# Gate arithmetic on 128 partitions, two prefix scans, an own place for a chunk's queries, and a newly searched order in an mLSTM with two MLP layers

## The chip, the cores and the metric

One core of one Trainium2 chip. The core has TensorE (PE; its weight loads are listed as PEld), VectorE (DVE), ScalarE (ACT), GpSimd (POOL) and SyncE (SP), which issues the fetches from HBM. The metric is the device time of one execution in microseconds, the median of several runs. Lower is better.

## The reference, cut to what matters

An mLSTM recurrence over 768 steps for 2 x 8 heads of width 40, with a running maximum m over the gates, then two MLP layers (320 to 2048 to 320) on its 1536 tokens.

```python
for t in range(S):
    m_new = np.maximum(f_gate[:, :, t] + m, i_gate[:, :, t])
    f_stab = np.exp(f_gate[:, :, t] + m - m_new)
    i_stab = np.exp(i_gate[:, :, t] - m_new)
    m = m_new
    C = f_stab * C + i_stab * outer(v_t, k_t)
    n = f_stab * n + i_stab * k_t
    y[:, :, t] = sigmoid(o_t) * (C @ q_t) / max(|n . q_t|, 1)
...
h = x @ w_in;  x = (h * clip(h + 3, 0, 6) / 6) @ w_out          # first layer
h = x @ w_in;  out = (h * tanh(log1p(exp(h)))) @ w_out          # second layer
```

## The kernel before

**Attention.** The sequence is cut into six chunks c of 128 steps, each of two halves of 64. `scan_gates` runs the maximum m along a row per (batch, head), 16 rows in all, with one scan; it takes chunk 0 alone, chunk 1 alone and chunks 2 to 5 together (`SCANS`). It then forms f + m(before) and subtracts m(after) from both gates, on those 16 partitions, in the tile gio (for chunk 1 on GpSimd, `pool_scan`). `gates(c)` transposes the two results of a chunk with the identity (tile pg), takes exp as a ratio of two sigmoids (tile ist), transposes the forget factor back (pf) and forms its running product in each half of 64 with one scan over 128 elements (pr): at the first element of each half the factor is put to 0 and its value is kept in the tile first, so that the scan starts anew there. For chunks 0 and 1 the decays are spread to 128 partitions by products with the identity (fb); for the others by a way through HBM (fzd). Then come, per chunk, the products of scores (s, L815), of the state (st, L942), of the state with the queries (x, L890) and of the decayed scores with the values (z, L985); `mixture(c)` puts them together and transposes the result (xp, L1041) into the input X of the first layer. X has three parts of two chunks each; two are made at the start, the third takes over memory that chunks 1 and 3 had used.

**Layers.** Weights are fetched in eight slots per layer, an in half (ri, 768 KB) and an out half (ro, 640 KB), through four raw buffers; ScalarE, VectorE and GpSimd split each into a high and a low part (`narrow`, `prep`: wh, wl, wd). The first layer runs chunks 0 and 1 (of X part 0) slot by slot (`step1`: ph, acc), then the parts 1 and 2 in wide blocks of 512 columns (`step1_wide`: phw, accw). The second layer (`step2`: qh, bcc) follows.

**Order.** The order of instructions on every engine is fixed when the program is built. All work is written as tasks with priorities (the lists in `P`, lowest first). `Flow` plays them through with estimated durations: whichever engine or buffer is free first takes the ready task of lowest priority, and the order so found is the program's. A fetch takes its turn on SyncE, which holds at most eight in flight. While TensorE would wait in this plan, `keep_warm` puts in products of zeros (tile pz), until chunk 1's result is there. The queries of a chunk (qke) share one buffer, `in_qke`, which is given back when the chunk's cross products and scores are done. Values and keys (kvo) have one place for chunks 1 and 3 and one for the others.

Of the kernel before, what the change touches and what calls it, by code (L numbers as in the profile page):

```python
# [16 lines left out]
ALU = mybir.AluOpType  # L17
# [25 lines left out]
    "const": [22, 11, 148],  # L43
    "gates": [81, 93, 41, 162, 127, 206],
    "load": [96, 281, 100, 227, 58, 130],
    "score": [9, 84, 243, 262, 211, 292],
    "value": [1, 29, 209, 138, 45, 241],
    "carry": [106, 73, 77, 59, 249, 250],
    "unit": [19, 171, 75, 86, 244, 228],
# [8 lines left out]
    ],  # L58
    "down2": [
        143, 60, 82, 259, 114, 54, 57, 63, 229, 156, 74, 6, 18, 44, 179, 139, 226, 173, 116, 155, 87, 183,  # L60
        203, 25, 72, 122, 53, 111, 115, 2, 151, 109, 27, 157, 3, 266, 263, 198, 24, 205, 32, 12, 88, 80,
        177, 89, 136, 90,
    ],
    "wide1": [
        140, 284, 67, 14, 33, 237, 185, 276, 235, 256, 288, 287, 215, 225, 248, 204, 191, 291, 184, 142, 17,
        79, 125, 144, 165, 34, 153, 39, 196, 293, 195, 102,
    ],
    "down1w": [
        35, 68, 290, 7, 105, 47, 30, 120, 251, 200, 297, 219, 50, 76, 124, 212, 152, 269, 16, 65, 99, 49,
        283, 26, 51, 15, 98, 94, 123, 37, 95, 277,  # L70
    ],
    "drain": [13, 217, 133, 126, 121, 56, 21, 48, 137, 71],
    "now": [4, 5],
# [13 lines left out]
    "pool_scan": [1, 0],  # L87
    "pe_low": [1, 1, 0, 0, 0, 0, 0, 0, 0, 0, 0, 0],
    "spread": [1, 1, 0, 0, 0, 0],
    "decay": [182, 253, 178, 141, 158, 104],  # L90
    "gload": [236, 40, 164, 175, 92, 181],
    "cross": [163, 83, 258, 103, 238, 66],
    "within": [214, 161, 36, 107, 112, 8],
# [50 lines left out]
class Flow:  # L144
# [4 lines left out]
    TO_PE, SWITCH = 0.13, 0.12  # L149
    TICK, COLUMNS = 10.24 / 3, 4000  # L150
    DMA = dict(rings0=2.0, slow=13e3, fast=20e3, until=3.0, start=1.9, end=0.5)

    def __init__(self):

        self.port = {DVE: 0.0, POOL: 0.0}
        self.engines = {PE: Engine(0.2), DVE: Engine(0.13), ACT: Engine(0.14), POOL: Engine(0.1), SP: Engine(0.0)}
        self.places = list(self.engines.values())
        self.now = 0.0
        self.rings, self.landed = [2.0] * 16, []
        self.tick, self.columns, self.fast = 0, 0.0, False  # L160
        self.fill, self.live, self.mode = None, 0, 0
# [76 lines left out]
    def transfer(self, place, t, size, n, issue):  # L238

        d = self.DMA  # L240
        rate = d["slow"] if t < d["until"] else d["fast"]
        for i in range(n):
            self.rings[i] = max(self.rings[i], t + d["start"]) + size / n / rate
# [30 lines left out]
    def grant(self, task, place, first):  # L274
# [5 lines left out]
        else:  # L280
# [4 lines left out]
            elif r[0] == PE:  # L285
                while self.fill and place.free + 0.45 < first:
                    self.fill()
                    place.free = self.products(place.free, 0.214, 512)
                mode = r[3] if len(r) > 3 else 0
                start = first + (self.SWITCH if mode != self.mode else 0.0)  # L290
# [11 lines left out]
def mlstm_mlp_kernel(ctx, tc, qk, kvon, gates_io, w1i, w1o, w2i, w2o, eyes, consts, out):  # L302
# [145 lines left out]
    for j in range(len(BLOCKS) - 1):  # L448
        new_x()
# [198 lines left out]
    first = gpool.tile([16, L], F32, tag="first", name="first")  # L648
# [8 lines left out]
    def scan_gates(i, c0, c1):  # L657
# [6 lines left out]
        on = i and P["pool_scan"][i - 1]  # L664
        eng = G if on else V
        for o, x, y, op in ((fgt, fgt, mt[:, a:z], ALU.add), (igt, igt, mt[:, a + 1 : z + 1], ALU.subtract),
                            (fgt, fgt, mt[:, a + 1 : z + 1], ALU.subtract)):
            yield flow.elementwise(on, 0.06 + 0.14 * n, 128 * n)
            tt(eng, o[:, r], x[:, r], y, op)
        flow.set(scanned[i])  # L670

    def gates(c):
# [5 lines left out]
        yield PE, 0.21, 128  # L678
        T.transpose(p[:, 0:16], fgt[:, q], ident[:16, :16])
        T.transpose(p[:, 16:32], igt[:, q], ident[:16, :16])  # L680
        g = istab[c] = gpool.tile([128, 32], F32, tag=f"ist{c}", name=f"ist{c}")
        s = gpool.tile([128, 32], F32, tag=f"s{c}", name=f"s{c}")
        yield ACT, 0.16
        A.activation(s, p[:, 0:32], AF.Sigmoid, scale=-1.0)
        A.activation(g, p[:, 0:32], AF.Sigmoid)
        flow.put(in_a)
        yield DVE, 0.27
# [22 lines left out]
        begins = pr.rearrange("r (a t) -> r a t", a=2)  # L710
# [9 lines left out]
        ends = begins[:, :, HL - 1]  # L720
# [39 lines left out]
    def loads(c, before):  # L760
# [105 lines left out]
    def cross(c):  # L866
# [44 lines left out]
        flow.put(in_qke)  # L911
# [452 lines left out]
```

## Time and profile before

| what | us |
|---|---|
| median of 3 runs | 434.56 (434.45 to 435.74) |
| the profiled execution | 434.39 |
| its span, first to last instruction | 432.6 |
| TensorE busy | 424.8 |
| VectorE busy | 303.0 |
| ScalarE busy | 268.9 |
| GpSimd busy | 60.0 |

The span is what the trace covers; 1.8 us of the execution's own time lie around it. Busy time is counted per engine and overlaps between engines. Matmuls are pipelined, so that TensorE's records overlap and a full stretch reads as fully busy.

### The profile page before, as it was taken

The numbers are of one execution on the slowest core, as the hardware profiler recorded it, in microseconds if no ns is written. First come the engines' busy times: TensorE is split into PE (matmuls) and PEld (weight loads), VectorE is DVE, ScalarE is ACT, GpSimd is POOL, SyncE is SP. The second block draws the span as 40 slices with busy tenths as digits, with TensorE's granted clock in tenths as the row PEclk, the third lists the DMA queues.
The fourth block names the chain that finished last, engine by engine and source line by source line (L and its number), as shares of the span: only waits on it lengthen the run. The fifth ranks groups of instructions, "written<-read, shape, count | busy, mean of one in ns | idle before, by whom it ended". The sixth has DMA issues, their size and how long they took to land.

```text
span 432.6 us, 9063 instructions
## 1 busy us (share of the span) xinstructions
PE 424.8 (98%) x3779; PEld 369.6 (85%) x3779; DVE 303.0 (70%) x532; ACT 268.9 (62%) x472; POOL 60.0 (14%) x54
## 2 busy tenths in 40 slices
PE   8999899999999999999999999999999999999996
PEld 6867899999998888887778888999999999899985
DVE  4989999999787322637976547766666666666664
ACT  5656676644443334069888358766686666767664
POOL 4010101181220134123036210000000000000000
PEclk9999999999999999999999999999999999999999
DMA  7958644651702027000782000000010000100001
GB/s 275 392 210 319 232 176 125 189 198 51 239 3 100 0 64 297 4 1 6 265 293 105 2 0 2 0 2 0 2 61 1 2 0 2 46 17 0 2 0 61
DMA packets 10040, 40.44 MB, mean 93 GB/s; under 512 B 2128, under 2 KB 3824, under 8 KB 9232
## 3 DMA queue, kind: packets, MB, share of 16 engines
q1 hardware_dynamic: 10000, 39.87, 25.8%
q8 instruction: 29, 0.48, 0.4%
q14 instruction: 11, 0.09, 0.1%
HBM read 37.64 MB, written 2.23 MB: 92 GB/s over the span
## 4 chain that ended last, share of the span: by engine, by line
PE 91%; DVE 4%; DMA 1%; ACT 1%; issue 1%; POOL 0%; DVEq 0%; ACTq 0%; POOLq 0%
PE qh L465 20%; PE accw L482 12%; PE phw L465 12%; PE acc L482 7%; PE ph L465 7%; PE bcc L1167 6%; PE bcc L1166 6%; PE bcc L1165 6%; PE pz L1198 4%; PE x L890 2%; PE s L815 1%; PE st L942 1%; DMA ri<-in_w2i 1%; PE z L985 1%; PE xp L1041 1%; PE fb L840 1%
## 5 line engine op out<-in xcount | busy, mean ns | idle before, releaser
L465 PE MATMUL qh<-x,wh 128*128 128x512 f32 x288 | 89.5, 392 | 0.0
L1116 DVE SCALAR_TENSOR_TENSOR u<-u,qh 128x512 f32<-128x512 f32 (+1 forms) x49 | 33.1, 676 | 39.1 <-ACT u L1114 39.1
L465 PEld LDWEIGHTS qh<-x,wh 128*128 128x128 f32 x288 | 52.3, 188 | 8.7
L1167 PE MATMUL bcc<-wd,gl 128*128 128x320 f32 x192 | 59.4, 309 | 0.2 <-DVE gl L1122 0.2
L1166 PE MATMUL bcc<-wd,gh 128*128 128x320 f32 x192 | 59.3, 309 | 0.0
L1165 PE MATMUL bcc<-wd,gh 128*128 128x320 f32 x192 | 59.3, 309 | 0.0
L465 PE MATMUL phw<-x,wh 128*128 128x512 f32 x192 | 58.9, 394 | 0.0
L1112 ACT ACTIVATE u<-u,two 128x512 f32<-128x512 f32 (+1 forms) x49 | 35.0, 715 | 30.8 <-DVE u L1110 30.7
L482 PE MATMUL accw<-ghw,wd 128*128 128x512 f32 x160 | 53.5, 399 | 0.0
L549 DVE SCALAR_TENSOR_TENSOR rw<-rw,phw 128x512 f32<-128x512 f32 x32 | 21.9, 686 | 38.4 <-ACT rw L547 38.2
L465 PEld LDWEIGHTS phw<-x,wh 128*128 128x128 f32 x192 | 35.7, 188 | 8.1
L547 ACT ACTIVATE rw<-phw,half 128x512 f32<-128x512 f32 x32 | 22.0, 689 | 26.5 <-PE phw L465 26.4
L482 PE MATMUL accw<-glw,wd 128*128 128x512 f32 x96 | 38.2, 398 | 0.2 <-DVE glw L309 0.2
L465 PE MATMUL qh<-x,wl 128*128 128x512 f32 x96 | 37.9, 395 | 0.0
L1165 PEld LDWEIGHTS bcc<-wd,gh 128*128 128x128 f32 x192 | 36.1, 188 | 2.1
L1166 PEld LDWEIGHTS bcc<-wd,gh 128*128 128x128 f32 x192 | 36.1, 188 | 1.9
L1106 ACT ACTIVATE u<-qh 128x512 f32<-128x512 f32 (+1 forms) x49 | 28.7, 587 | 14.3 <-PE qh L465 14.2
L1167 PEld LDWEIGHTS bcc<-wd,gl 128*128 128x128 f32 x192 | 36.1, 188 | 0.4 <-DVE gl L1122 0.4
L1122 DVE SCALAR_TENSOR_TENSOR gl<-u,gh 128x512 fp32r<-128x512 f32 (+1 forms) x49 | 33.1, 675 | 3.4 <-ACT gh L1120 3.3
L482 PEld LDWEIGHTS accw<-ghw,wd 128*128 128x128 f32 x160 | 29.5, 188 | 6.5
L1110 DVE SCALAR_TENSOR_TENSOR u<-u 128x512 f32<-128x512 f32 (+1 forms) x49 | 33.4, 681 | 1.6
L465 PE MATMUL ph<-x,wh 128*128 128x256 f32 x192 | 34.2, 288 | 0.0
(153 smaller groups left out, 838.7 us busy)
## 6 DMA issues: line engine op xcount, KB each, us to landing
ri<-in_w1i SPq DMA_DIRECT2D x8, 768.0 KB, 6.4
qke<-in_qk SPq DMA_DIRECT2D x6, 1024.0 KB, 5.0
ri<-in_w2i SPq DMA_DIRECT2D x8, 768.0 KB, 6.1
kvo<-in_kvon SPq DMA_DIRECT2D x6, 968.0 KB, 7.6
ro<-in_w1o SPq DMA_DIRECT2D x8, 640.0 KB, 5.2
ro<-in_w2o SPq DMA_DIRECT2D x8, 640.0 KB, 5.0
fb<-fzd SPq DMA_DIRECT2D x4, 512.0 KB, 4.3
out<-ot SPq DMA_DIRECT2D x12, 160.0 KB, 1.8
```

The source lines that it names most:

```text
L465: T.matmul(ph, a, b, start=(i == 0), stop=(i == len(seq) - 1))
L482: T.matmul(acc[k], a, b, start=start, stop=stop, skip_group_check=True)
L547: A.activation(r, ph, AF.Relu, bias=half, scale=1.0 / 6.0)
L549: V.scalar_tensor_tensor(out=r, in0=r, scalar=1.0, in1=ph, op0=ALU.min, op1=ALU.mult)
L1106: A.activation(u, ph, AF.Exp)
L1110: V.scalar_tensor_tensor(out=u, in0=u, scalar=2.0, in1=u, op0=ALU.add, op1=ALU.mult)
L1112: A.activation(u, u, AF.Ln, bias=two)
L1116: V.scalar_tensor_tensor(out=u, in0=u, scalar=0.5, in1=ph, op0=ALU.subtract, op1=ALU.mult)
L1122: V.scalar_tensor_tensor(out=gl, in0=u, scalar=-2.0, in1=gh.bitcast(F32), op0=ALU.mult, op1=ALU.subtract)
L1165: T.matmul(acc, a, hi, start=st, stop=False)
L1166: T.matmul(acc, a, lo, start=False, stop=False)
L1167: T.matmul(acc, b, hi, start=False, stop=sp)
```

## The change

- The gate subtractions leave `scan_gates`. `gates(c)` now transposes f, i, m before and m after (four transposes instead of two), copies the two m to SBUF on ScalarE, and adds and subtracts them on VectorE on 128 partitions, reading PSUM. The `pool_scan` entry goes.
- The running product is two scans of 64 elements, each started with 1.0, over a tile of zeros (nothing); the copy into first and the memset go.
- Chunk 1's queries are fetched into the memory of X part 1 (tile x1) instead of the shared buffer. Only part 0 of X is made at the start; part 1 is made when chunk 1 is done.
- The first gates are a task of their own with priority 0, ahead of the identity.
- `Flow` plays fetches with other constants (rate, start, end, sizes), gives each filler product at least 0.25 us and has two switch times. All priority lists are new.

```diff
 P = {
-    "const": [22, 11, 148],
+    "const": [55, 264, 205],
...
-    "load": [96, 281, 100, 227, 58, 130],
+    "load": [11, 262, 266, 59, 218, 45],
...
-    "prep0": [55, 62, 166, 0, 85, 160, 168, 52, 192, 149, 271, 213, 230, 234, 289, 285],
-    "prep1": [218, 169, 274, 220, 280, 282, 10, 135, 20, 172, 232, 38, 261, 189, 210, 194],
+    "prep0": [128, 75, 176, 132, 42, 109, 177, 116, 246, 53, 271, 261, 282, 274, 278, 280],
+    "prep1": [281, 273, 203, 187, 257, 138, 36, 193, 222, 259, 182, 235, 179, 192, 115, 253],
...
-    "now": [4, 5],
+    "first": [0],
+    "now": [7, 8],
...
-    "pool_scan": [1, 0],
...
-    TO_PE, SWITCH = 0.13, 0.12
+    TO_PE, SWITCH = 0.13, (0.12, 0.21)
...
-    DMA = dict(rings0=2.0, slow=13e3, fast=20e3, until=3.0, start=1.9, end=0.5)
+    FILL = 0.25
+    DMA = dict(first=1.5, rate=24e3, start=1.7, end=0.9)
...
-    for j in range(len(BLOCKS) - 1):
-        new_x()
+    new_x()
...
-        on = i and P["pool_scan"][i - 1]
-        eng = G if on else V
-        for o, x, y, op in ((fgt, fgt, mt[:, a:z], ALU.add), (igt, igt, mt[:, a + 1 : z + 1], ALU.subtract),
-                            (fgt, fgt, mt[:, a + 1 : z + 1], ALU.subtract)):
-            yield flow.elementwise(on, 0.06 + 0.14 * n, 128 * n)
-            tt(eng, o[:, r], x[:, r], y, op)
...
-        yield PE, 0.21, 128
-        T.transpose(p[:, 0:16], fgt[:, q], ident[:16, :16])
-        T.transpose(p[:, 16:32], igt[:, q], ident[:16, :16])
+        yield PE, 0.4, 256
+        for i, x in enumerate((fgt[:, q], igt[:, q], mt[:, q], mt[:, c * L + 1 : (c + 1) * L + 1])):
+            T.transpose(p[:, 16 * i : 16 * i + 16], x, ident[:16, :16])
...
-        yield ACT, 0.16
-        A.activation(s, p[:, 0:32], AF.Sigmoid, scale=-1.0)
-        A.activation(g, p[:, 0:32], AF.Sigmoid)
+        yield ACT, 0.1
+        A.copy(s, p[:, 32:64])
+        yield DVE, 0.08
+        tt(V, p[:, 0:16], p[:, 0:16], s[:, 0:16], ALU.add)
+        yield DVE, 0.1
+        tt(V, g.rearrange("t (x r) -> t x r", x=2), p[:, 0:32].rearrange("t (x r) -> t x r", x=2),
+           s[:, 16:32].unsqueeze(1).to_broadcast([128, 2, 16]), ALU.subtract)
         flow.put(in_a)
+        yield ACT, 0.25
+        A.activation(s, g, AF.Sigmoid, scale=-1.0)
+        A.activation(g, g, AF.Sigmoid)
...
-        yield DVE, 0.08, True
-        V.tensor_copy(first.rearrange("r (a t) -> r a t", a=2)[:, :, 0:1], begins[:, :, 0:1])
-        yield DVE, 0.03, True
-        V.memset(begins[:, :, 0:1], 0.0)
-        yield DVE, 0.33, True
-        V.tensor_tensor_scan(out=pr, data0=pr, data1=first, initial=0.0, op0=ALU.mult, op1=ALU.add)
+        for a in range(2):
+            half_of = pr[:, a * HL : (a + 1) * HL]
+            yield DVE, 0.2, True
+            V.tensor_tensor_scan(out=half_of, data0=half_of, data1=nothing, initial=1.0, op0=ALU.mult, op1=ALU.add)
...
-        yield in_qke
-        t["qke"] = apool.tile([128, B, 2, 4, L], F32, tag="qke", name=f"qke{c}")
-        yield SP, 852e3, ev["qk"], 13, 0.54
+        if c == 1:
+            flat = xpool.tile([128, 3072], F32, tag="x1", name="qke1")[:, 0 : 16 * L]
+            t["qke"] = flat.rearrange("p (b y h t) -> p b y h t", b=B, y=2, h=4)
+        else:
+            yield in_qke
+            t["qke"] = apool.tile([128, B, 2, 4, L], F32, tag="qke", name=f"qke{c}")
+        yield SP, 1049e3, ev["qk"], 16, 0.5
...
-        flow.put(in_qke)
+        if c != 1:
+            flow.put(in_qke)
...
-                yield ends[3]
+                yield ends[1 if c // 2 == 1 else 3]
...
-        yield SP, 16e3, (ev := Event())
-        SY.dma_start(out=gio[:, :, 0:L], in_=gates_io[:, :, 0:L])
...
-    def scan_first(ev):
+    def first_gates():
+        yield SP, 64e3, (ev := Event())
+        SY.dma_start(out=gio[:, :, 0:L], in_=gates_io[:, :, 0:L])
         yield ev
         yield from scan_gates(0, *SCANS[0])
...
+        flow.add(P["first"][0], first_gates())
```

## Rows read from the trace of the kernel before

**Rows 1.** The page's line of engines: busy us, share, instructions.
```profile
PE 424.8 (98%) x3779; PEld 369.6 (85%) x3779; DVE 303.0 (70%) x532; ACT 268.9 (62%) x472; POOL 60.0 (14%) x54
```

**Rows 2.** Table of stages: stretch, length, busy time of engines, clock, DMA share, GB/s.
```profile
10.00:20.00 10.00, 10.00 (x189) 7.79 (x187) 9.07 (x21) 7.24 (x17) 0.00 (x0) 1.00 1.02 408
20.00:30.00 10.00, 8.95 (x200) 7.03 (x196) 8.81 (x18) 4.05 (x7) 2.05 (x2) 1.00 0.50 175
140.00:160.00 20.00, 20.00 (x91) 16.20 (x90) 6.84 (x11) 8.32 (x16) 3.87 (x3) 1.00 0.02 2
```

**Rows 3.** The same table for the filler tile pz alone, first 40 us (PE, PEld).
```profile
0.00:40.00 40.00, 19.45 (x61) 12.43 (x61) 1.00 0.82 311
```

**Rows 4.** Instructions in order of time: start, duration, engine, line, operation, out<-in.
```profile
1.19 0.72 SPq L1182 DMA_DIRECT2D gio<-in_gates_io  x1
...
5.23 0.74 SPq L767 DMA_DIRECT2D qke<-in_qk  x1
...
8.31 0.23 PE L679 MATMUL pg<-eye,gio 16*128 16x16 f32 x1
...
9.33 0.31 DVE L309 TENSOR_TENSOR ist<-ist,s 128x32 f32<-128x32 f32 x1
...
18.94 1.16 PE L815 MATMUL s<-qke 40*64 40x64 f32 x64
...
23.20 1.13 PE L942 MATMUL st<-kvo 64*64 64x41 f32 x64
...
40.00 0.50 PE L465 MATMUL ph<-x,wh 128*128 128x256 f32 x2
...
120.08 0.56 DVE L309 TENSOR_TENSOR x<-xp,x 128x384 fp32r<-128x384 f32 x1 [0.23 <-ACT x L1053]
```

**Rows 5.** Fetch issues: how many, KB each, us from issue to landing (median).
```profile
gio<-in_gates_io SPq DMA_DIRECT2D x1, 16.0 KB, 4.1
...
eye<-in_eyes SPq DMA_DIRECT2D x1, 128.0 KB, 3.8
...
out<-ot SPq DMA_DIRECT2D x12, 160.0 KB, 1.8
```

**Rows 6.** Time to landing by tile: queries (qke), values (kvo), weights in (ri).
```profile
DMA to landing us min/median/max: 4.7/5.0/9.6
...
DMA to landing us min/median/max: 4.7/7.6/11.1
...
DMA to landing us min/median/max: 4.1/6.2/10.1
```

**Rows 7.** Table of stages for VectorE alone: length, busy (instructions), clock, DMA.
```profile
20.00:100.00 80.00, 75.42 (x147) 1.00 0.57 203
80.00:100.00 20.00, 19.47 (x32) 1.00 0.53 178
0.00:120.00 120.00, 105.62 (x209) 1.00 0.61 217
```

**Rows 8.** The chain that ended last, in order of time: start, length, what.
```profile
122.40 1.82 PE phw L465 x8
124.22 1.92 PE acc L482 x16
```

**Rows 9.** Tile ist: the gate product, ns min/median/max, first and last start.
```profile
L309 DVE TENSOR_TENSOR ist<-ist,s x6: 155/192/1590, 9.3 to 62.1; 128x32 f32<-128x32 f32 x6
```

**Rows 10.** VectorE's groups to 125 us: count | busy us, mean ns | idle before.
```profile
L367 DVE SCALAR_TENSOR_TENSOR ri<-ri,top 128x768 uint32<-128x768 uint32 x9 | 8.5, 943 | 0.0
L367 DVE SCALAR_TENSOR_TENSOR ro<-ro,top 128x640 uint32<-128x640 uint32 x9 | 8.2, 923 | 0.5 <-ACT top L365 0.5
...
L712 DVE COPY first<-pr 16x2 f32<-16x2 f32 x6 | 0.9, 150 | 0.2 <-ACT pr L708 0.2
```

**Rows 11.** Tile gio on VectorE: ns min/median/max, first and last start, forms.
```profile
L309 DVE TENSOR_TENSOR gio<-gio,mt x6: 272/474/674, 5.9 to 45.7; 16x128 f32<-16x128 f32 x3, 16x512 f32<-16x512 f32 x3
L662 DVE TENSOR_TENSOR_SCAN mt<-gio,mt x3: 467/475/1269, 5.4 to 38.8; 16x128 f32<-16x128 f32 x2, 16x512 f32<-16x512 f32 x1
```

More of the change, by code (lines that the diff above doesn't have):

```diff
@@ L42 @@
 P = {
-    "const": [22, 11, 148],
-    "gates": [81, 93, 41, 162, 127, 206],
-    "load": [96, 281, 100, 227, 58, 130],
[L46 to L49, printed above, removed]
[4 rows of a table removed]
+    "const": [55, 264, 205],
+    "gates": [22, 111, 150, 191, 293, 151],
+    "load": [11, 262, 266, 59, 218, 45],
+    "score": [15, 267, 270, 81, 285, 251],
+    "value": [9, 207, 283, 24, 297, 196],
+    "carry": [26, 152, 54, 276, 43, 226],
+    "unit": [108, 136, 72, 56, 5, 18],
[4 rows of a table added]
     "up2": [
[3 rows of a table removed]
[3 rows of a table added]
     ],
     "down2": [
-        143, 60, 82, 259, 114, 54, 57, 63, 229, 156, 74, 6, 18, 44, 179, 139, 226, 173, 116, 155, 87, 183,
-        203, 25, 72, 122, 53, 111, 115, 2, 151, 109, 27, 157, 3, 266, 263, 198, 24, 205, 32, 12, 88, 80,
-        177, 89, 136, 90,
+        65, 103, 216, 27, 173, 68, 16, 30, 39, 12, 154, 144, 234, 25, 91, 185, 23, 82, 21, 28, 71, 87, 77,
+        157, 48, 31, 110, 233, 129, 74, 190, 32, 100, 2, 120, 4, 99, 88, 133, 175, 189, 125, 158, 131, 122,
+        245, 210, 236,
     ],
     "wide1": [
-        140, 284, 67, 14, 33, 237, 185, 276, 235, 256, 288, 287, 215, 225, 248, 204, 191, 291, 184, 142, 17,
-        79, 125, 144, 165, 34, 153, 39, 196, 293, 195, 102,
+        180, 181, 295, 70, 114, 97, 198, 121, 244, 250, 167, 217, 215, 34, 147, 172, 145, 76, 98, 141, 60,
+        161, 213, 94, 89, 188, 40, 228, 231, 93, 171, 44,
     ],
     "down1w": [
-        35, 68, 290, 7, 105, 47, 30, 120, 251, 200, 297, 219, 50, 76, 124, 212, 152, 269, 16, 65, 99, 49,
-        283, 26, 51, 15, 98, 94, 123, 37, 95, 277,
-    ],
-    "drain": [13, 217, 133, 126, 121, 56, 21, 48, 137, 71],
-    "now": [4, 5],
+        49, 6, 101, 130, 258, 119, 159, 230, 105, 69, 260, 90, 79, 163, 252, 29, 299, 290, 123, 19, 165, 78,
+        104, 139, 3, 178, 63, 46, 83, 86, 247, 127,
+    ],
+    "drain": [95, 225, 294, 92, 1, 298, 102, 199, 155, 51],
+    "first": [0],
+    "now": [7, 8],
     "window": [0.05],
@@ L86 @@
     "pe_rest": [0, 0, 0, 0, 0, 1, 0, 1, 0, 1, 0, 0, 0, 0, 0, 0],
-    "pool_scan": [1, 0],
     "pe_low": [1, 1, 0, 0, 0, 0, 0, 0, 0, 0, 0, 0],
     "spread": [1, 1, 0, 0, 0, 0],
[L90 to L93, printed above, removed]
+    "decay": [14, 183, 269, 208, 41, 241],
+    "gload": [256, 13, 284, 164, 248, 237],
+    "cross": [202, 57, 206, 20, 227, 67],
+    "within": [265, 268, 37, 62, 52, 239],
     "act_rows": [0, 0, 1, 0, 0, 1],
@@ L158, in __init__ @@
         self.now = 0.0
-        self.rings, self.landed = [2.0] * 16, []
+        self.rings, self.landed = [self.DMA["first"]] * 16, []
         self.tick, self.columns, self.fast = 0, 0.0, False
@@ L240, in transfer @@
         d = self.DMA
-        rate = d["slow"] if t < d["until"] else d["fast"]
         for i in range(n):
-            self.rings[i] = max(self.rings[i], t + d["start"]) + size / n / rate
+            self.rings[i] = max(self.rings[i], t + d["start"]) + size / n / d["rate"]
         end = max(self.rings[:n]) + d["end"]
@@ L287, in grant @@
                     self.fill()
-                    place.free = self.products(place.free, 0.214, 512)
+                    place.free = max(place.free + self.FILL, self.products(place.free, 0.214, 512))
                 mode = r[3] if len(r) > 3 else 0
-                start = first + (self.SWITCH if mode != self.mode else 0.0)
+                start = first + (self.SWITCH[mode > 0] if mode != self.mode else 0.0)
                 self.mode = mode
@@ L647, in mlstm_mlp_kernel @@
     fzd, istab, pend_sc, prefix = {}, {}, {}, {}
-    first = gpool.tile([16, L], F32, tag="first", name="first")
+    nothing = gpool.tile([16, HL], F32, tag="nothing", name="nothing")
     scanned = [Event() for _ in SCANS]
@@ L719, in gates @@
         yield DVE, 0.1, True
-        ends = begins[:, :, HL - 1]
+        ends = pr.rearrange("r (a t) -> r a t", a=2)[:, :, HL - 1]
         tt(V, dd, cst[:, CM : CM + 8].unsqueeze(2).to_broadcast([16, 8, 2]), ends.unsqueeze(1).to_broadcast([16, 8, 2]), ALU.mult)
@@ L1180, in start @@
         flow.add(P["now"][0], keep_warm())
-        yield SP, 16e3, (ev := Event())
-        SY.dma_start(out=gio[:, :, 0:L], in_=gates_io[:, :, 0:L])
         yield SP, 131e3, have["ident"]
         SY.dma_start(out=eye[:, 0:256], in_=eyes)
-        flow.add(P["now"][0], scan_first(ev))
         flow.add(P["now"][0], spread_ident())
@@ L1228, in clear @@
         yield POOL, 0.2
-        G.memset(first, 0.0)
+        G.memset(nothing, 0.0)
         flow.set(have["clear"])
@@ L1236, in constants @@
     def constants():
-        yield SP, 7e3, have["cst"]
+        yield SP, 28e3, have["cst"]
         SY.dma_start(out=cst, in_=consts)
     def other_gates():
-        yield SP, 82e3, have["gates"]
+        yield SP, 328e3, have["gates"]
         SY.dma_start(out=gio[:, :, L:], in_=gates_io[:, :, L:])
```

1 line of the change is left out of this document (removed), and 10 rows, old and new, of the table P.

## The prediction

> **What bounds the kernel now.** I read the page's engine line first, then the table of stages, the filler tile by itself, the start in order of time, the fetches, and last VectorE's load and prices. TensorE is busy 424.8 us of the span [rows 1], so whatever costs TensorE time behind the start is paid in full, and a gain must come from time in which TensorE is busy for nothing. In the table of stages [rows 2] the reader is to see 20.00 of 20 us even in the middle, at a granted clock of 1.00 (2.4 GHz) in every row. But the filler tile pz, products of zeros that keep the array going, holds 19.45 us of the first 40 [rows 3]. So the kernel has a start of 40.0 us, until the first product of the first MLP layer (ph) [rows 4], and about half of it is filler; from there on TensorE is fed.
>
> What makes the start so long? In order of time [rows 4]: the first gates are issued at 1.19 and land 4.1 us later [rows 5], at 5.3; the gate transposes run at 8.31; the product that finishes the gate runs from 9.33 to 9.64; the scores of chunk 0 at 18.94; its state product at 23.20; ph at 40.00. The queries' fetch was issued at 5.23 and took 9.6 us, the longest of its kind [rows 6], so it had landed at 14.8. The scores ran 4.1 us after that: TensorE's order was fixed ahead, and filler and other products stood before them. Beside this chain VectorE is nearly full: 75.42 of 80 us from 20 to 100, 94% [rows 7]. It is the second bound: it does the attention, half of the weight preparation and half of the activations, and the attention up to chunk 3 must be through before the wide block (phw) starts at 122.40 [rows 8].
>
> **The change part by part.** *Gates first.* The 16 KB of gates go out before everything (first has priority 0), at 0.74 instead of 1.19 (SyncE's first issue stands at 0.74 today), with no 640 KB of weights ahead. Landing is between 1.8 us (the quickest kind, an output of 160 KB) and 4.1 us (this fetch today) after issue [rows 5]; I take 3.5, nearer to the start's own fetches, so 4.3 instead of 5.3. The identity is second and lands by 5.0 (3.8 us from an issue at about 1.2). The three subtractions on 16 partitions between scan and transposes go. The transposes start at about 5.1 instead of 8.31.
>
> *Gates on 128 partitions.* Between transposes and finished gate stand three more steps per chunk: a copy on ScalarE, an addition 128x16 and a subtraction 128x32 on VectorE that read PSUM. The trace has no such pair; the nearest row is the gate product of 128x32, 155 to 192 ns as a rule and 1590 ns once [rows 9]. I take 0.15 and 0.18, as the median is what it is nearest to. With an estimated 0.2 for the copy and hand-overs of 0.1 to 0.2 each, the chain grows by 0.6 to 1.3 us; I take 0.9. The gate of chunk 0 is then ready at 5.1 + 1.3 + 0.9 = 7.3 instead of 9.6 (1.3 is 8.31 to 9.64). If each new operation met the 1590 ns of one in six, that would be 2 x 1.4 us more on VectorE, which the lower VectorE load of a rival below covers. TensorE pays two more transposes per chunk. One such record lasts 0.23 us [rows 4], but they overlap; I take 0.1 each (0 to 0.23). Chunks 0 and 1 hide this in filler; chunks 2 to 5 stand where TensorE is full: 4 x 2 x 0.1 = 0.8 us lost.
>
> *Two prefix scans.* The copy into first goes (0.9 us in all [rows 10]), a small memset too, and one scan of 128 becomes two of 64. A scan of 128 takes 0.47, one of 512 takes 1.27 [rows 11], so 2.08 ns per element and 0.20 us fixed: halving costs those 0.20 once more. VectorE in all: removed 3 x 0.27 + 3 x 0.67 = 2.8 (subtractions on gio [rows 11]) + 0.9 = 3.7 us; added 6 x (0.33 + 0.20) = 3.2; net 0.5 us less. GpSimd also loses three subtractions for chunk 1, for which no one waited.
>
> *Place for chunk 1's queries, and the new order.* Today chunk 1's queries wait for the one buffer until chunk 0 has read it. Now they go to the memory of X[1] at once; X[1] is made when chunk 1 is done, long before chunk 2's result needs it, so this costs nothing. SyncE's order follows from the priority lists (lowest first): gates, identity, chunk 0's queries and values (11), weights in 2 (42), out 4 (53), constants, out 0 (75), out 2 (109), then chunk 1's queries and values (262), then the other gates (264). Today four weight fetches stand before chunk 0's queries. So these are issued at about 2.0 and 2.5; with the medians of their kinds, 5.0 and 7.6 us [rows 6], they land at 7.0 and 10.1 instead of 14.8 and 17.1. The bounds are 4.7 for either and 9.6 and 11.1, which came behind weights. From the gate at 7.3, decay products, two scans and two multiplications by the scores (about 1.2 us each but the last) bring chunk 0 to 12.5, the state product to about 13.7 instead of 23.20. The rest, 23.20 to 40.00, is 16.8 us of chain and shared VectorE; kept as it is, ph could start at 30.5.
>
> *Weights.* Slot 0's out half is the eighth fetch; its in half comes once one of the four raw buffers is free, at about 16. Ahead of it then stand 7.0 MB of fetches, at the 408 GB/s of 10 to 20 us [rows 2] until 19.5 or so, then its own 2 us and a latency of 1 to 2: landed at 22 to 24, prepared about 4 us later, at 26 to 28. It is not the last to come. First ph at 31: 9.0 us earlier.
>
> *What VectorE gives back.* TensorE keeps only what VectorE can follow. Of VectorE's 105.6 us up to 120 [rows 7] all but 0.1 lie behind the landing at 5.3; at 94% that ends at 5.3 + 105.5/0.943 = 117.2. After: 4.3 + 105.0/0.943 = 115.6, 1.6 earlier. If the second layer's slot 0 (priorities 281 and 273, about last) moves behind the wide block's start, its two shifts, 0.94 + 0.92 [rows 10], go too: 113.6, 3.6 earlier, which I take, since VectorE has room there (6.84 of 20 us [rows 2]). Besides, chunk 3's result is ready at 120.6 today [rows 4], while first-layer products still run until 122.40 and again from 124.22 to 126.1 [rows 8]: 3.7 us of slack, of which I count 2.0. Kept: 5.6 of the 9.0.
>
> **Sum.** 434.39 (the profiled execution; 1.8 around its span; the runs' median is 434.56) - 5.6 + 0.8 = 429.6 us. Bounds: 434.39 - 9.0 + 0.8 = 426.2 if VectorE follows fully; 434.39 - 1.6 + 0.8 = 433.6 if nothing moves out and no slack is used.
>
> **Rivals.** *VectorE takes nearly all back.* If its load falls from 94 to 92%, because small operations meet the 1590 ns case more often, the work ends at 4.3 + 103.1/0.92 = 116.4, 0.8 earlier than today's 117.2; the transposes eat that: 434.4, no change. For it: 94% over 80 us; against it: the slack, and a wide block with room.
>
> *Weights behind chunk 1's data (slower).* The in halves of slots 1 and 3 stand at 176 and 177, after the out halves. Chunk 1's 2.04 MB go ahead of them: 5.0 us at 408 GB/s. The trace has such a case: the longest weight fetch took 10.1 us, against a median of 6.2 [rows 6]. If slots 1 and 3 each hold TensorE for 5.0 us, with ph at 31, the time is 434.4 - 9.0 + 10.0 + 0.8 = 436.2. It decides once these waits pass 8.2 us together. Against it: slot 3 is needed some 15 us after slot 0, and the fetches run at 175 GB/s from 20 to 30 us [rows 2], so there is room to catch up. The Trainium skill (DMA: Bandwidth & Descriptors, "Queues, rings and completion order") says that each ring consumes its descriptors in order. By that rule every early fetch of chunk 1 delays each weight fetch behind it, so that slots 1 and 3 come late and the time is this rival's 436.2 if TensorE has nothing else to do; the 10.1 us agree as to the delay, and no row shows TensorE waiting for a weight.
>
> *The full gain.* With VectorE loaded at 97%, as from 80 to 100 us [rows 7], the work ends at 4.3 + 103.1/0.973 = 110.3, 6.9 earlier; with the slack the start is the limit: 426.2.
>
> *The gates are not the point.* If queries and values land later than the gate anyway, the gate part brings nothing and only its costs remain; the order's gain stands without it. This changes the reason, not the time.
>
> **How the numbers follow.** Forecast (427.5 to 432) 0.52; full gain or more 0.12; between forecast and no change (432 to 433.1) 0.11; VectorE takes it back 0.13; weights late, or another place where the fixed order meets the chip badly, 0.12. About 0.3%, 1.3 us, is what a measurement of this kernel (434.45 to 435.74 in three runs) can tell from no change. Faster 0.75, within 0.13, slower 0.12. The range runs from 425.8, just under the full gain, into the no-change case, 434.2.
>
> **What would show it.** Filler should fall from 19.45 to about 13 us and the first ph move from 40.0 to between 30 and 34; the scores should run near 11, not 18.94; phw should start some 5 to 6 us earlier. From ph on TensorE should stay full: a wait of ph for the weights (wh or wl) would mean the slower rival, one for VectorE's gl or oc the first. The prediction is wrong if ph starts early and phw does not, or if the granted clock shows a stretch at 0.5 (1.2 GHz) where filler was left out.

## The result, and the profile after

The changed kernel takes 439.64 us (median; 435.33 to 444.45), the kernel before, run beside it, 434.47 (432.81 to 438.75). The ratio is 1.0094 with a 95% interval of 1.0066 to 1.0121: slower by 0.94%, where 429.6 and faster was forecast. The ratio is taken over runs in the fast state alone, which leaves out the two longest of the changed kernel (443.56 and 444.45); by the medians of all runs the loss is 5.2 us, by this ratio 4.1. The profiled execution took 440.11 us against 434.39.

The page's lines of engines and of the granted clock, of the changed kernel (a digit of the clock is one of 40 slices, here 10.96 us each):

```profile
PE 425.4 (97%) x3759; PEld 368.0 (84%) x3759; DVE 299.7 (68%) x532; ACT 269.3 (61%) x478; POOL 61.7 (14%) x51
...
PEclk9769999999999999999999999999999999999999
```

Its table of stages, with columns as in [rows 2], and the row of the filler tile alone for the first 40 us (PE, PEld, clock):

```profile
10.00:20.00 10.00, 5.40 (x52) 3.64 (x55) 7.49 (x13) 6.29 (x12) 2.03 (x2) 0.84 1.02 391
20.00:30.00 10.00, 10.00 (x150) 7.31 (x142) 5.41 (x16) 4.15 (x13) 0.00 (x0) 0.50 0.94 363
30.00:40.00 10.00, 9.43 (x175) 7.43 (x171) 9.45 (x21) 8.17 (x17) 0.00 (x0) 0.98 0.31 97
...
0.00:40.00 40.00, 10.18 (x27) 6.01 (x27) 0.83 0.75 281
```

In order of time, the instructions that answer to [rows 4], with the fetches of chunk 0's queries, of the first out weights and of chunk 1's queries:

```profile
0.74 0.73 SPq L1207 DMA_DIRECT2D gio<-in_gates_io  x1
2.13 0.43 SPq L768 DMA_DIRECT2D qke<-in_qk  x1
3.55 0.67 SPq L357 DMA_DIRECT2D ro<-in_w1o  x1
5.73 0.44 SPq L768 DMA_DIRECT2D qke<-in_qk  x1
...
4.17 0.39 PE L673 MATMUL pg<-eye,gio 16*128 16x16 f32 x2
7.76 1.16 PE L816 MATMUL s<-qke 40*64 40x64 f32 x64
9.97 1.86 PE L1197 MATMUL pz<-zeros 128*128 128x512 f32 x7
16.43 0.56 PE L394 MATMUL pw<-ro,eye 128*128 128x320 f32 x1 [4.59 <-DVE ro L367]
19.26 1.93 PE L944 MATMUL st<-kvo 64*64 64x41 f32 x64
28.45 1.95 PE L987 MATMUL z<-kvo,fb 64*64 64x41 f32 x64
41.05 0.28 PE L464 MATMUL ph<-x,wh 128*128 128x256 f32 x1
125.05 0.62 PE L464 MATMUL phw<-x,wh 128*128 128x512 f32 x2
```

The reader is to see a good beginning and a hole behind it. The transposes run at 4.17 instead of 8.31 and the scores at 7.76 instead of 18.94, earlier than forecast (near 11). The last seven products of zeros ahead of the hole then go by in 1.86 us, and from 11.8 to 16.43 TensorE waits 4.59 us for the shift of the first out weights (ro). After that the granted clock is 0.50 (1.2 GHz) for all of 20 to 30 us, while TensorE's records fill every microsecond. It comes back after 30 us. In that stretch the state product takes 1.93 us, against 1.13 for the same 64 products in [rows 4]. The first ph starts at 41.05, not at 31; phw at 125.05 instead of 122.24 ([rows 8] enters it at 122.40, behind its first product).

In three stretches, by the first ph, phw and qh (the second layer's first product; 250.98 before, 256.72 after): up to ph 40.00 and 41.05; ph to phw 82.24 and 84.00; phw to qh 128.74 and 131.67. Behind qh both take the same 181.6, to the end of the span. One chunk's state products (64 of them, 1.1 us) moved from the first stretch into the second, and chunk 4's scores and prefix products (1.2 and 0.65 us) from the second into the third. Without these moves the change costs 2.1, 2.5 and 1.1 us.

### The profile page after: what moved, and what is told of

It reads as the page before. It is cut to its first block, busy times and chain, and to the rows that moved or that the text cites. A ratio compares the mean times of both kernels' runs of the same rounds, so it can differ in the third digit from the quotient of the medians.

```text
span 438.3 us, 9026 instructions
## 1 busy us (share of the span) xinstructions
PE 425.4 (97%) x3759; PEld 368.0 (84%) x3759; DVE 299.7 (68%) x532; ACT 269.3 (61%) x478; POOL 61.7 (14%) x51
## 4 chain that ended last, share of the span: by engine, by line
PE 79%; DVE 9%; DMA 4%; ACT 3%; issue 2%; POOL 1%; SPq 0%; ACTq 0%; DVEq 0%
PE qh L464 20%; PE accw L481 11%; PE phw L464 11%; PE bcc L1169 6%; PE bcc L1168 6%; PE bcc L1167 6%; PE acc L481 5%; PE ph L464 5%; DMA ri<-in_w1i 3%; PE z L987 1%; DMA ri<-in_w2i 1%; PE st L944 1%; PE x L891 1%; ACT top L365 1%; PE pw L394 1%
## 5 line engine op out<-in xcount | busy, mean ns | idle before, releaser
L464 PE MATMUL ph<-x,wh 128*128 128x256 f32 x192 | 35.2, 290 | 0.3 <-DVE wh L309 0.3
```

What stands on the lines that cost most here:

```text
L464: T.matmul(ph, a, b, start=(i == 0), stop=(i == len(seq) - 1))
```

## The experiments

Theories: **A**, the filler was used up early, so that a wait of TensorE lay uncovered and the clock fell while the chain of the start ran on TensorE. **B**, the new order itself costs it (weights' steps ahead of chunk 0's), whatever the clock. **C**, the new gate arithmetic costs it. **D** came later: VectorE takes back what the start gives. "New order" is the changed kernel's order of instructions, kept to the instruction except for the edit shown; "old order" is that of the kernel before. The edits leave the planned order of everything else as it was.

| run | order | median us | ratio to before, 95% | first ph | ph to phw | phw to qh |
|---|---|---|---|---|---|---|
| e1 filler over the hole | new | 436.98 | 1.0048 [1.0025, 1.0072] | 36.31 | 84.66 | 132.06 |
| e13 e1, decay ahead of weights | new | 436.79 | 1.0042 [1.0013, 1.0071] | 35.91 | 84.61 | 130.76 |
| e14 e1, eight VectorE steps out | new | 438.14 | 1.0103 [1.0057, 1.015] | 36.53 | 83.73 | 131.54 |
| e7 e1, old gates and scan | new | 441.31 | 1.0158 [1.0124, 1.0192] | 37.14 | 88.37 | 132.25 |
| e3 less filler | old | 435.89 | 1.0023 [0.9993, 1.0053] | 40.54 | 82.20 | 130.48 |
| e2 new gates and scans | old | 438.09 | 1.0073 [1.0046, 1.01] | 39.99 | 83.97 | 130.23 |
| e9 new gates alone | old | 437.63 | 1.0082 [1.0064, 1.0099] | 40.12 | 84.00 | 130.35 |
| e17 e9, copy on VectorE | old | 438.11 | 1.0087 [1.006, 1.0115] | 40.33 | 83.83 | 130.45 |
| e16 two more transposes | old | 435.93 | 1.0017 [0.9992, 1.0041] | 39.75 | 82.62 | 130.37 |
| e8 two prefix scans alone | old | 434.21 | 1.001 [0.9987, 1.0033] | 39.25 | 82.23 | 128.96 |
| e10 gates first alone | old | 434.55 | 1.0011 [0.9994, 1.0028] | 39.44 | 82.23 | 129.58 |
| e6 own place for queries | old | 434.74 | 1.0004 [0.9977, 1.0031] | 38.62 | 82.22 | 130.49 |
| e11 e6, e8 and e10 together | old | 434.94 | 1.0016 [0.9998, 1.0034] | 40.21 | 82.22 | 130.41 |
| e15 eight VectorE steps out | old | 434.60 | 0.9999 [0.9975, 1.0022] | 39.70 | 82.23 | 130.50 |

The last three columns are from one profiled execution each. The kernel before had medians of 434.17 to 434.92 in these comparisons; its own row would read 40.00, 82.24 and 128.74. Most runs have 10 to 12 executions, e7 and e9 six, e14 four.

**e1, filler over the hole.**

```diff
 def fill():
-    T.matmul(pz, zeros[:, 0:128], zeros, start=True, stop=True)
+    fills[0] += 1
+    for _ in range(1 + 19 * (fills[0] == 17)):
+        T.matmul(pz, zeros[:, 0:128], zeros, start=True, stop=True)
```

> The changed kernel with 19 more products of zeros (about 4.6 us at 0.24 us each) put into TensorE's order just ahead of the first low-part weight product (pw), nothing else moved. Theory A (the filler was used up early, a wait of 4.6 us stood uncovered, the clock fell to 0.5 from 16.8 to 30.5 us, and the chain of chunk 0 ran late on a slow TensorE): mean clock 1.000, first ph at 36 to 38.5 instead of 41.05, time back to 0.998 to 1.004 of the kernel before. Theory B (the order itself: weight steps ahead of chunk 0's steps on ScalarE and VectorE, waiting for fetches, whatever the clock): clock 1.000 too, but ph still at 40 to 41 and phw at 124 to 125, ratio 1.007 to 1.010. Theory C (the new arithmetic costs it): as B.

Its table of stages for 10 to 30 us:

```profile
10.00:20.00 10.00, 9.41 (x103) 7.13 (x103) 7.63 (x14) 6.41 (x13) 2.05 (x2) 1.00 1.02 395
20.00:30.00 10.00, 9.42 (x220) 7.36 (x219) 9.37 (x28) 7.35 (x19) 0.00 (x0) 1.00 1.00 402
```

The granted clock is 1.00 in every row of the first 40 us. The product that stands behind the hole (pw) runs at 16.35, against 16.43 in the changed kernel, so the filler shortened no wait; from there on the two differ in TensorE's speed. ph started at 36.31, 4.74 us earlier, and phw at 120.97, 4.08 us earlier than in the changed kernel. So theory A holds about half of the loss (the ratio of 1.0048 is just above the 1.004 that it allowed), and what the products of zeros gave back is the clock. The changed kernel's own 20 executions point the same way: the one whose mean clock was 1.000 took 435.33 us, the four at 0.990 to 0.992 took 436.18 to 437.45, and the fifteen at 0.973 to 0.984 took 438.55 to 444.45. Left are 2.4 us to the kernel before (436.98 against 434.59).

**e3, the old order with less filler.**

```diff
+    fills[0] += 1
+    if fills[0] <= 26:
         T.matmul(pz, zeros[:, 0:128], zeros, start=True, stop=True)
```

> The kernel before with its last 35 of 61 filler products left out (those behind 10 us), order untouched. Theory A (filler holds the clock and with it the start's chain): the clock shows a stretch at 0.5 between 12 and 40 us, mean below 0.985, and the time rises by 2 to 6 us (ratio 1.005 to 1.014). Theory B: TensorE only waits where it computed zeros, the time stays within 0.4%.

Its table of stages (columns as above):

```profile
20.00:30.00 10.00, 6.79 (x174) 6.32 (x171) 8.77 (x19) 3.59 (x7) 2.05 (x2) 0.56 0.44 160
30.00:40.00 10.00, 8.53 (x125) 5.91 (x125) 8.77 (x16) 7.68 (x20) 0.00 (x0) 0.76 0.99 402
```

The clock was low for about as long (from about 21.2 to 34.8 us; in the changed kernel from 16.8 to 30.5), and ph came 0.54 us later, not 4.7. The time stayed within 0.4%, which the expectation had given to theory B: a low clock alone costs little in this order. TensorE still waits in this order while it is slow (6.79 and 8.53 of 10 us busy), so slow products can run into time that was free; in the new order it is busy 10.00 of 10, which leaves none.

**e6, chunk 1's queries early, in the old order** (fetched into X part 1's memory right behind chunk 0's values).

```diff
 SY.dma_start(out=kvo[:, 0:KVO], in_=kvon[c * L : (c + 1) * L])
+if c == 0:
+    SY.dma_start(out=tiles[1]["qke"], in_=qk[1])          # in the memory of x1
```

> The kernel before with only chunk 1's queries in their own place, fetched right behind chunk 0's values, at about 6.5 us instead of 27.2; the order of all else untouched. If 1 MB more ahead of the weights is what hurts (part of theory B): the weight fetches issued at 9 and 15 us land about 2.6 us later, ph moves to 41 to 43, ratio 1.004 to 1.008. Theory A: no hole in the filler opens, within 0.3%.

No change that can be told (ratio 1.0004): 1 MB ahead of the weights does not hurt here. phw was 1.40 us early in the profile and qh late, though: see the last section.

**e2 and e9, the new gate arithmetic in the old order.** e2 takes the change's lines for gates and prefix scans, e9 those for the gates alone.

> The kernel before, its order and filler untouched, with only the gate arithmetic on 128 partitions and the two prefix scans: the new steps are written in where the old ones stood, the old subtractions are left out. Theory C (the parts cost it): slower by 0.5% or more. Theories A and B: within 0.3%, at most 0.8 to 1.1 us for the extra transposes, ph at 39.5 to 40.5.

> The kernel before with the gate arithmetic on 128 partitions alone (four transposes, a copy, two VectorE operations), one prefix scan. Theory C says that this holds the 3.2 us of the experiment with both: 437.5 to 438, phw 1.5 to 2 us later than before. If it is what the prediction counted, 0.8 us of transposes and nothing else: 435.2 to 435.6. TensorE's gate transposes should go from 1.23 us to about 2.0 in all in either case.

e9 holds all of e2's cost: 3.5 us (437.63 against 434.17). Its tile pg (ns min/median/max, first and last start), and a wait of ScalarE and one of TensorE in order of time:

```profile
L683 ACT COPY s<-pg x6: 167/180/185, 8.3 to 62.1; 128x32 f32<-128x32 f32 x6
L309 DVE TENSOR_TENSOR pg<-pg,s x6: 149/179/183, 8.6 to 62.6; 128x16 f32<-128x16 f32 x6
L309 DVE TENSOR_TENSOR ist<-pg,s x6: 191/192/193, 8.8 to 62.8; 128x32 f32<-128x32 f32 x6
...
63.05 0.23 ACT L687 ACTIVATE s<-ist 128x32 f32<-128x32 f32 x1 [0.82 <-DVE pr L717]
63.78 0.33 PE L1044 MATMUL xp<-eye,kvo 128*128 128x128 f32 x1 [0.66 <-ACT kvo L1037]
```

The steps last what was forecast. But ScalarE, in its fixed order, stands at the sigmoids (0.82 us at 63.05) until VectorE has done its two new steps, and the copy that xp needs stands behind them. The releaser named there is a small memset; VectorE's new subtraction, at 62.76, ends at the same 62.95. Of the 3.5 us the profile places 1.8 between ph and phw (84.00 against 82.24). The 1.6 more between phw and qh are no more than this stretch varies by itself (last section), so where the other half of the cost lies is not shown.

**e16 and e17, which part of the gates.**

```diff
 T.transpose(p[:, 16:32], igt[:, q], ident[:16, :16])
+T.transpose(p[:, 32:48], mt[:, q], ident[:16, :16])                            # e16: read by nothing
+T.transpose(p[:, 48:64], mt[:, c * L + 1 : (c + 1) * L + 1], ident[:16, :16])
...
-A.copy(s, p[:, 32:64])                                                         # e17, on e9
+V.tensor_copy(s, p[:, 32:64])
```

> The kernel before with two more transposes per chunk beside the two that it has, of running maxima into columns that nothing reads; arithmetic and order stay the old ones. If the cost of the gates on 128 partitions (3.4 us in the old order) is TensorE's own, as the prediction's 0.8 us would have it at least in part, phw comes 0.5 to 0.9 us later and the time goes to 435.0 to 435.8. If the cost is the hand-overs between ScalarE and VectorE (theory C), the transposes alone cost 0.3 to 0.8 us: 434.5 to 435.1.

> The kernel before with the gate arithmetic on 128 partitions, the copy out of PSUM on VectorE instead of ScalarE (one change of engine fewer per chunk). If hand-overs make the 3.4 us, the waits of ScalarE stay (its two sigmoids still wait for VectorE) but a step of 0.2 to 0.3 us goes: 436.5 to 437.3. If the place in the old order alone matters (new steps put into queues that were ordered without them), no change from 437.6.

The transposes alone: 0.17% or 0.7 us (the interval reaches from -0.3 to 1.8; by the medians 1.2), ph to phw 82.62 instead of 82.24. One change of engine fewer brings nothing. That leaves some 2.8 of the 3.5 us (1.7 to 3.8 by the same interval). The likely cause is new steps in queues that were ordered without them, since the steps are short and one change of engine fewer does not help; no run shows it directly.

**e8, e10 and e11, the small parts.** e8 has the change's two prefix scans; e10 issues the first gates ahead of all; e11 is e6, e8 and e10 together.

> The kernel before with the two prefix scans of 64 alone. If the arithmetic's cost is a chain on VectorE, the scans without the copy and the memset take it down: 0.3 us less per chunk, 434.0 to 434.5. If a cost of the new arithmetic lies here (two scans of 0.3 to 0.4 each), 435 to 436. My prediction counted them as part of a net gain of 0.5 us of VectorE.

> The kernel before with the first fetch of gates issued ahead of everything and nothing else moved. If the gates are not the point (a rival of the prediction), no change: 434.2 to 434.9, first ph at 39.5 to 40.0. If the start's chain hangs on them, ph comes up to 1 us earlier and the time goes to 433.5.

> The kernel before with the gates fetched first, the two prefix scans and the own place of chunk 1's queries together, old gate arithmetic and old order. Each alone moved the time by less than 0.3% but brought phw forward in its profile (by 0.5 to 1.4 us). If these add up, phw at 119.5 to 120.5 and 432 to 433. If the second layer's weights, which ScalarE waits for between 213 and 220 us, take back whatever comes earlier, no change: 434 to 435.

None moves the time, nor do all three: the gains of 0.5 to 1.4 us at phw in single profiles don't add up (122.43 in e11, against 122.24 before).

**e7, the old arithmetic in the new order, with e1's filler.**

```diff
+for o, x, y, op in ((fgt, fgt, mt[:, a:z], ALU.add), ...):      # back in scan_gates
+    tt(eng, o[:, r], x[:, r], y, op)
...
-A.copy(s, p[:, 32:64])
+A.activation(s, p[:, 0:32], AF.Sigmoid, scale=-1.0)
+A.activation(g, p[:, 0:32], AF.Sigmoid)
```

> The changed kernel with the 19 products of zeros of the first experiment and with the gate arithmetic and the single prefix scan of the kernel before, in the changed kernel's order. Theory A and C together (half of the loss is the start without filler, the rest the new arithmetic): the 2.1 us that were left at 436.7 to 437.0 go nearly all, 434.5 to 435.5, first ph near 36.3 as with the filler alone, phw 1 to 2 us earlier than there (119 to 120). Theory B (the new order costs it behind the start, whatever the arithmetic): the subtractions come back on 16 partitions, the gate is ready about 1 us later, and the time stays at 436.5 to 437.5.

Slower than e1 (441.31 against 436.98, 4.3 us). Both theories named in the expectation fall: C as a price that simply adds, and B as an order that costs the same with either arithmetic. In order of time TensorE now waits for the subtractions on 16 partitions and for what hangs on the gate:

```profile
51.94 0.23 PE L676 MATMUL pg<-eye,gio 16*128 16x16 f32 x1 [1.25 <-DVE gio L309]
...
70.23 0.35 PE L722 MATMUL pf<-dd,cst 16*104 16x16 f32 x2 [1.90 <-DVE dd L309]
```

Its table of stages behind the second wait:

```profile
70.00:80.00 10.00, 9.77 (x72) 9.58 (x72) 7.58 (x17) 4.90 (x11) 2.06 (x1) 0.83 0.69 199
```

So part of the 4.3 us is the clock again: behind the wait of 1.90 us the granted clock of this profile falls to 0.50 for some 3.4 us. Three of e7's six executions had a mean clock of 0.981 to 0.992; the three at 0.995 or more average 439.5, 2.6 us above e1's average of 436.9. Each order fits the arithmetic it was made for: the new gates cost 3.5 us in the old one and save 2.6 to 4.3 in the new one.

**e14 and e15, VectorE relieved in both orders.** The eight multiplications of decay by scores of chunks 2 to 5 are left out, so that their attention is not the reference's.

```diff
-tt(V, part, part, t["s"][p], ALU.mult)
+if c < 2:
+    tt(V, part, part, t["s"][p], ALU.mult)
```

> The changed kernel with the 19 products of zeros, and without the eight multiplications of the decay by the scores of chunks 2 to 5 on VectorE (0.65 us each, 5.2 us in all; the attention of these chunks is then not the reference's). Theory D (with the hole covered, VectorE takes back what the earlier start gives: it was 2.8 us less busy up to 20 us than in the kernel before and has to do that later): 3 to 5 us faster than with the filler alone, 432 to 434, phw at 116 to 118, the waits of pf, x and ph on VectorE gone. Theory B (TensorE waits by the fixed order, not by VectorE's load): less than 1 us faster, 436 to 437.

> The kernel before without the same eight multiplications on VectorE (5.2 us; not the reference's attention for chunks 2 to 5). If VectorE's load of 94% bounds the kernel before up to phw, as the prediction had it, 2 us or more faster, 432 and below, phw at 119 to 120. If TensorE is the only bound there (it waits for VectorE 1.1 us in all in that stretch), it stays within 1.2 us: 433.3 to 434.5.

The 5.2 us are those of the whole kernel. Between ph and phw stand six of the eight multiplications in the old order and four in the new one, and VectorE's busy time there falls from 76.74 to 72.74 us and from 74.58 to 72.55.

In the old order ph to phw stays at 82.23 and the time at 434.60. So VectorE did not bound the kernel before there, though it was busy 94% of the time [rows 7]. In the new order the same stretch shortened by 0.93 us; the time did not fall (438.14, but of four executions, at mean clocks of 0.984 to 1.000, with an interval 0.9% wide). Three of the waits of TensorE on VectorE that theory D wanted gone are still there, nearly as long as in e1 (0.43, 0.44 and 0.89 us, listed further down):

```profile
41.36 0.74 PE L464 MATMUL ph<-x,wh 128*128 128x256 f32 x4 [0.54 <-DVE wh L309]
43.49 1.13 PE L892 MATMUL x<-c,qke 40*64 40x41 f32 x60 [0.43 <-DVE c L309]
66.47 0.35 PE L720 MATMUL pf<-dd,cst 16*104 16x16 f32 x2 [0.87 <-DVE dd L309]
```

So these waits hang on where steps stand and not on VectorE's load, and theory D falls as the main cause. With 2.0 us taken off the stretch it is a weaker test than the expectation, which counted all 5.2, took it for.

**e13, the decay ahead of the weights.** VectorE and ScalarE in e1, in order of time:

```profile
12.01 0.74 ACT L865 ACTIVATE kvo<-kvo 128x640 f32<-128x640 f32 x1
14.23 0.93 ACT L365 CAST top<-ro 128x640 f16<-128x640 bf16 x1 [1.49 <-DMA ro<-in_w1o]
15.03 0.24 ACT L708 COPY pr<-pf 16x128 f32<-16x128 f32 x1
...
15.30 0.28 DVE L713 TENSOR_TENSOR_SCAN pr<-pr,nothing 16x64 f32<-16x64 f32 x1 [1.86 <-ACT pr L708]
```

The copy pr has had its input since pf's product at 9.82, but it stands behind the copy of out weights (top) that waits for a fetch, and VectorE waits 1.86 us for it. e13 lets pr and ul go first.

```diff
-A.copy(top, upper)                          # o0_4; o0_0's goes behind o0_4's split
+later["ul"].append(copy)                    # issued behind ul's copy
...
-V.scalar_tensor_tensor(out=e, in0=e, scalar=13, in1=top, ...)
+later["fb"].append(shift)                   # behind the first multiplication
```

> The changed kernel with the 19 products of zeros, and chunk 0's copies of the decay ends (pr and ul) moved ahead of the copy of the first out weights on ScalarE, the first multiplication ahead of the shift on VectorE; the second out slot's copy follows the first one's split. With the filler alone ScalarE held pr and ul from 13.0 to 15.0 for a weights fetch that landed at 14.2. Theory B (the fixed order at the start costs it): VectorE's multiplications start near 14.0 instead of 16.2, the state product near 17.8 instead of 18.6, first ph 0.6 to 1.0 us earlier (35.3 to 35.7), and the time falls by as much, 436.0 to 436.5. If the start is set by the weights and not by chunk 0's chain, ph stays within 0.3 us of 36.3 and the time at 436.7 to 437.2.

```profile
13.37 0.22 ACT L861 COPY ul<-fb 128x16 f32<-128x16 f32 x1 [0.61 <-DVE fb L856]
14.36 0.92 ACT L371 CAST top<-ro 128x640 f16<-128x640 bf16 x1 [0.77 <-DMA ro<-in_w1o]
...
13.62 0.69 DVE L309 TENSOR_TENSOR fb<-fb,s 128x512 f32<-128x512 f32 x1
```

The multiplication starts at 13.62 and the state product at 18.06 instead of 18.59, but ph gains only 0.40 us, less than theory B had (0.6 to 1.0), and the median can't be told from e1's. This hold is real and is worth some tenths, because two others stay. VectorE still waits for the same copy, with the shift ahead of its second multiplication (16.26) and of the values' (16.93):

```profile
15.32 0.83 DVE L374 SCALAR_TENSOR_TENSOR ro<-ro,top 128x640 uint32<-128x640 uint32 x1 [1.00 <-ACT top L371]
```

And TensorE's products of the out weights stand ahead of the state product.

## Why the prediction was wrong

The forecast was 9.0 us at the first ph, 5.6 of them kept, 0.8 paid. The measured time is 10.0 us above the forecast. Two steps failed on the way to ph: the state product came 4.9 us late for a reason that the sum left out, and the filler was treated as free, which cost another 4.7 us at ph and 2.7 of the time (e1). A third failed behind ph: with the clock at full the start was 3.7 us shorter, but only 1.3 of them were left at phw (120.97 against 122.24) and none in the time. The steps in order:

**Gates, right in kind.** They landed at 2.8 (forecast 4.3) and the transposes ran at 4.17 (5.1). From the transposes at 4.17 to the end of the gate product at 6.45 it is 2.28 us against 1.33 before: 0.95 more, for 0.9. The new steps have medians of 0.17 to 0.18 us, for 0.15 to 0.2; the rare 1590 ns did not show. Transposes 0.8: 0.7 in e16, whose interval includes zero. The two scans cost nothing that can be told (e8). What the sum left out is that a step may cost more by its place in a queue than by its length (e9).

**Queries and scores, right.** The queries landed at 7.2 (forecast 7.0), the values at 11.4 (10.1), the scores ran at 7.76 (near 11); the own place costs nothing that can be told (e6).

**"The state product to about 13.7", the first failed step.** It ran at 18.59 even with filler, because I added up chunk 0's own operations and did not ask what else stands between them on the queues of ScalarE, VectorE and TensorE: the out weights, whose fetch landed 10.7 us after issue. The 10.7 could have been estimated: with it 3.6 MB were under way, which at the 417 GB/s of 5 to 10 us is an estimated 8.7 us. e13 shows that ScalarE's part of the hold is worth 0.5 us at the state product (18.06); the other parts are read from the queues and were not taken away one by one. The median of the four such fetches issued in the first 16 us of the changed kernel is 10.9 us:

```profile
ro<-in_w1o SPq DMA_DIRECT2D x4, 640.0 KB, 10.9
```

**Weights, right in the conclusion.** Slot 0's in half was issued at 21.06 in e1 (forecast about 16) and its last part (wh) done at 33.55 (26 to 28). The transposed input (xp) came later, at 36.01, so the weights were not the last to come.

**"The rest ... is 16.8 us ... kept as it is, ph could start at 30.5", the second failed step, about half of the loss.** With the clock at full it was 17.7 us (18.59 to 36.31 in e1), near the forecast; in the changed kernel 21.8 (19.26 to 41.05). I treated the filler as time in which "TensorE is busy for nothing" and took it to shrink with the start. It also holds the clock. The plan had fixed the places of its products; TensorE ran ahead of the plan, used them up by 11.8 us and met its first long wait with none left. `Flow`, played through with the changed kernel's lists, shows by how much: it takes TensorE as slow until about 17 us and puts the seven products from 13.6 to 16.6, at 0.43 us each, right up to pw at 16.62. On the chip TensorE's products ran at full speed from about 6.6 us on, and the seven stood from 9.97 to 11.83, while pw had to wait for its weight until 16.43. The same plan has ph at 36.3, where e1 has 36.31: the forecast of 30.5 was 5.8 us ahead of the kernel's own plan, which the prediction did not look at. The condition that the prediction named for being wrong, "a stretch at 0.5 (1.2 GHz) where filler was left out", is what came; no rival had a price for it. The Trainium skill (TensorE: Matmul & The Clock Gate, "Part 1: The HAM clock gate") says that slow is the array's default and that activity releases it; the trace agrees in that the wait of 4.59 us stands right before the stretch at 0.50, that the clock rose again while TensorE was busy, and that the first products of zeros take 0.63 us each, against 0.39 later.

**"It is the second bound": wrong in this sum.** The sum took VectorE at 94% from 4.3 us on. It was busy 10.42 of the first 20 us in e1, as it waited for fetches and for other engines, and 13.22 in the kernel before. The first fence below is e1, the second the kernel before (length, VectorE busy, clock, DMA):

```profile
0.00:20.00 20.00, 10.42 (x24) 1.00 0.87 334
```

```profile
0.00:20.00 20.00, 13.22 (x35) 1.00 0.90 335
```

And e15 shows that its load does not set phw in the old order. Whether it sets the stretch from the state product to ph is open: in e1 VectorE is busy 16.94 of these 17.72 us, and no run took work off it there.

**"Kept: 5.6 of the 9.0", the third failed step.** What the start gave back was not kept by VectorE's room but lost behind ph. In e1 the start is 3.7 us shorter (2.6 without the moved state products), but ph to phw costs 3.2 more than in the old order once the moves are counted (84.66 - 82.24 + 1.85 - 1.1). Both stretches, the kernel before first, then e1:

```profile
40.00:122.24 82.24, 81.10 (x1270) 77.70 (x1267) 76.74 (x146) 46.93 (x95) 18.17 (x14) 1.00 0.49 165
```

```profile
36.31:120.97 84.66, 82.29 (x1270) 77.93 (x1268) 74.58 (x147) 49.32 (x102) 21.19 (x13) 1.00 0.45 158
```

TensorE is idle for 2.37 us instead of 1.14. The waits of e1 in order of time:

```profile
41.03 0.74 PE L464 MATMUL ph<-x,wh 128*128 128x256 f32 x4 [0.43 <-DVE wh L309]
43.16 1.13 PE L891 MATMUL x<-c,qke 40*64 40x41 f32 x60 [0.44 <-DVE c L309]
44.46 0.50 PE L481 MATMUL acc<-gh,wd 128*128 128x256 f32 x2 [0.17 <-ACT gh L551]
45.19 0.38 PE L481 MATMUL acc<-gl,wd 128*128 128x256 f32 x1 [0.23 <-DVE gl L309]
...
56.84 0.33 PE L1043 MATMUL xp<-eye,kvo 128*128 128x128 f32 x1 [0.21 <-ACT kvo L1036]
...
67.17 0.35 PE L720 MATMUL pf<-dd,cst 16*104 16x16 f32 x2 [0.89 <-DVE dd L309]
```

These are the 2.4 us. The old order has one wait there:

```profile
52.12 0.38 PE L482 MATMUL acc<-gl,wd 128*128 128x256 f32 x1 [1.14 <-DVE gl L309]
```

So waits make 1.2 of the 3.2. The other 2.0 are time in which TensorE is busy: 0.5 in the transposes of chunks 2 to 5 (tile pg there: 1.50 against 1.00 us), up to 0.7 in a pair of products (pj) that the old order runs behind phw, and the rest was not placed. VectorE's load explains a part at most: it is busy for less of it than in the old order (74.58 of 84.66 us against 76.74 of 82.24), and taking 2.0 us off it gave 0.9 (e14).

**The rivals.** "Weights behind chunk 1's data" had the mechanism, TensorE waiting for a weight, in the wrong place: the fetch that it waited for went out at 3.55, ahead of chunk 1's at 5.73. "Another place where the fixed order meets the chip badly" was part of the 0.12, without a number. "The gates are not the point" holds in the old order (e10) and not in the new one (e7).

**Open.** Which of the waits behind ph could be taken away together was not tried, nor a plan that takes TensorE as fast from 6.6 us on and so would have set the filler where the chip needed it. And no run here beat the kernel before.

## What to carry to other kernels

Filler products are not waste to be subtracted: before moving work ahead of them, find the longest wait that is left without any, and price the stretch behind it at the low clock if TensorE is full there. Where a plan fixes the order, play it through first: it names the places of the filler and a time for each stage, to be set against the trace. When an order is fixed per engine, a chain's time is not the sum of its own operations: at each step look for the instruction ahead of it on that queue and for what that one waits for. A busy share of 94% is no proof of a bound; only taking work away from the engine tells.

## What the runs showed of the hardware that was not expected

The low clock costs according to what stands in it: a stretch of like length moved ph by 0.54 us (e3) and by 4.74 (the changed kernel against e1).

The tables' clock reads 1.00 from the first row on, but up to about 6.2 us the products of zeros last 628 ns as a rule, against 389 to 398 behind that, in the kernel before as in the changed one. So the first rows of the clock are to be checked against the products' own durations.

Between phw and qh the same instructions took 128.74 to 130.49 us in profiles of old-order kernels that left this stretch alone (the kernel before and e6 are the two ends). By the starts of their products, their distance from the kernel before stays the same up to about 217 us and changes then. ScalarE's waits from 200 to 222 us show one reason, first in the kernel before, then in e6 (sum, times, longest):

```profile
ACT top L365 <- DMA ri<-in_w2i: 0.7, 1, 0.7
```

```profile
ACT top L365 <- DMA ro<-in_w2o: 1.7, 2, 1.3
```

The second layer's weights came later in e6, relative to the work around them. So 1 to 1.7 us at the end of one profile can be the fetches of that execution; that they are the whole of it was not shown.
